# PSUM banks assigned by role, with value tiles formed one slot after their gates, in a fused attention and ReGLU kernel

## The chip, the cores and the metric

The kernel runs on one core of one Trainium2 chip. The metric is the device time of one execution in microseconds; the kernel before takes 866.84 us, the median of 3 runs (865.91 to 870.33). The profile is of one execution of its own.

The engines are named as in the profile: PE is TensorE (matmuls into PSUM, which has 8 banks here), PEld its weight loads, ACT is ScalarE, DVE is VectorE, POOL is GpSimd, SP issues the DMAs. Each engine takes its instructions in the order in which the program gives them to it, and waits for others by semaphores.

## The reference

The input `x` holds 4 batches of 12416 rows of 128. Each batch first attends from 32 fixed rows to its own rows, which gives `h` (32 × 128); then each row of `x` attends to `h`; the result goes through a gated feed-forward layer of width 1536.

```python
def mab(q, kv):
    s = scale * (q @ kv.transpose(0, 2, 1))
    s = s - s.max(-1, keepdims=True)
    a = np.exp(s)
    a /= a.sum(-1, keepdims=True) + 1e-09
    return a @ kv
h = mab(I, x)
y = mab(x, h)
...
gate = np.maximum(y @ w_gate, 0.0)
val = y @ w_val
return gate * val @ w_out
```

## The kernel before, in words

**Algebra.** The second attention and the layer's input weights are merged: for each batch the kernel computes `hgv`, that is `h @ w_gate` and `h @ w_val`, kept for 32 rows each, twice (row groups 0 and 64 the gate, 32 and 96 the value). A gate tile of 128 features by 512 rows of `x` is then one matmul of K = 32 between `hgv` and the unnormalised exps `p2`. Since the layer is a ReLU times a linear term, the softmax's denominator comes out as its square, and is applied to the finished output (L502, twice `z`).

**Tiling.** A batch is 97 tiles of 128 rows: 12 pairs of blocks (a block is 512 rows), and a rest of one tile. A pair has 12 slots, one per 128 of the 1536 features; the rest has 3 slots of four features' tiles each. A batch is therefore 147 slots, and everything that is planned has a slot number `at`.

**A slot** (L577 to L619). For both blocks `k` of the pair, TensorE forms a gate tile and a value tile (L584, four matmuls of K = 32 and N = 512, one in each of the four row groups). Then come the fillers of this slot (`fill[at]`) and some projections (`out_work`). ScalarE turns a gate tile into `g16` (ReLU, L610), VectorE multiplies `g16` by the value tile in PSUM into `gv` (L615). The list `post[at]`, follow-ups of earlier fillers on all engines, is worked off after the first block's ReLU and multiply, ahead of the second's.

**Projections.** For each block a chain of 12 matmuls (L480, `out_step`) sums `wo` times `gv` in one bank. `out_work` spends a budget of 2 projections per slot (1 in the rest), on the oldest chain, as far as its `gv` tiles are two slots old. One slot after a chain's last matmul ScalarE copies the bank to `oT` (L491), one later SP transposes it by DMA, then GpSimd scales (L502) and SP stores.

**Fillers.** `ev_s2` plans the scores of the next pair (L164, two matmuls) and a slot later their exp `p2` on ScalarE (L174); `ev_z2` the denominators (L183, four small matmuls) and a slot later their reciprocal on VectorE (L191). `plan_phase1` spreads the next batch's first attention over the slots of the current one: loads on SP, casts on GpSimd (L339), DMA transposes, first-phase scores `s1` (L359) with their exps (L369), the sums for `h` (`h_part`, L425, seven of them, followed by `sums`, `join` and `finish_h`), and the three pieces of `hgv` (L140). Batch 0 does this ahead of all slots, in a prologue of its own.

**Banks.** All PSUM tiles have one tag, `ring`, with 8 buffers of a bank each (L57). A tile takes a buffer that is free or will be the soonest in the order that the compiler plans; a matmul waits until the bank's last reader is done.

Of the kernel before, what the change touches and what calls it, by code (L numbers as in the profile page):

```python
# [9 lines left out]
FP32 = mybir.dt.float32  # L10
FP16 = mybir.dt.float16
# [6 lines left out]
def kernel(  # L18
# [20 lines left out]
    P = 128  # L39
# [47 lines left out]
    indT = constp.tile([P, M], FP16, name="indT")  # L87
    indT_ps = ring("indT_ps", [P, M], FP16)
    nc.tensor.transpose(indT_ps, ind16, eye16[:M, :M])
# [46 lines left out]

    def hgv_pe(hT, k):
        ps = ring("hgv_ps")
# [20 lines left out]
    def s2_pe(hT, xT, pr):  # L159
        ps = ring("s2_ps")  # L160
        if pr < NPAIR:
            for k in range(2):
                t0 = (2 * pr + k) * TPB
                nc.tensor.matmul(  # L164
                    ps[64 * k : 64 * k + 64, :], hT, xTs(xT, t0, TPB), start=True, stop=True
                )
# [12 lines left out]
    def z2_pe(p2, pr):  # L179
        ps = ring("z2_ps", [P, TPB, 2], FP32)  # L180
        if pr < NPAIR:
# [17 lines left out]
    xT = {}  # L199
    hT_ps = ring("hT_ps", [P, M], FP32)  # L200
    z1_ps = ring("z1_ps", [P, CT, M], FP32)
    x32s = {}
# [16 lines left out]
    for q in range(NCH):  # L219
# [16 lines left out]
        for a in range(t0, t1, 8):  # L236
            e = min(a + 8, t1)
            ps = ring("xT_ps", [P, 8, P], FP16)
            for t in range(a, e):
# [8 lines left out]
        p1s[q] = p1  # L248
        ps = ring("s1_ps", [P, CT, M], FP32)
        for t in range(t0, t1):  # L250
# [9 lines left out]
    s2 = s2_pe(hT, xT, 0)  # L260
    pss = [hgv_pe(hT, k) for k in range(3)]
    p2 = s2_exp(s2, 0)
# [38 lines left out]
    for b in range(B):  # L301
        for pr in range(NPAIR + 1):
            if (b, pr) == (0, 0):
                ev_z2(0, 0, 1)
                continue
            if pr == 0:
# [12 lines left out]

    def plan_phase1(b):  # L320
# [11 lines left out]
        for q in range(NCH):  # L332
# [21 lines left out]

            def s1(q=q, at=at + 18):
                ps = ring("s1T_ps")
                for r in range(4):
# [24 lines left out]
            if q < NQ:  # L382
                fill[at + 18].append(s1)

        at = at0 + NFF * NCH + 7

        def s1_rest(at=at):
            ps = ring("s1T_ps")
            nc.tensor.matmul(ps[0:M, 0:P], indT, xTs(s["xT"], NT - 1, 1), start=True, stop=True)
# [21 lines left out]

        at = at0 + NFF * (NQ + 2)

        def h_part(q):
            if q == 0:
                s["h_ps"] = ring("h_ps", [P, P], FP32)
            ps = s["h_ps"]
# [14 lines left out]

        for q in range(NQ + 1):
            fill[at + q].append(lambda q=q: h_part(q))

# [8 lines left out]

        post[at + NQ + 2].append(sums)

        def join():
            ps = ring("hz_ps", [P, 2, M], FP32)
            nc.tensor.matmul(ps[:, 0, :], s["hp"], stackI, start=True, stop=True)
# [5 lines left out]

            post[at + NQ + 5].append(dve)

        fill[at + NQ + 4].append(join)
        for k in range(3):

            def mk(k=k, a=at + NQ + 8 + 2 * k):
                ps = hgv_pe(s["hT"], k)
                post[a + 1].append(lambda: hgv_evac(s["hgv"], ps, k))

            fill[at + NQ + 8 + 2 * k].append(mk)

# [6 lines left out]
    def out_step(at):  # L473
# [4 lines left out]
        if i == 0:  # L478
            c["ps"] = ring("o_ps")
        nc.tensor.matmul(  # L480
# [42 lines left out]

    carry = 0.0

    def out_work(at, budget):
        nonlocal carry
        carry += budget
        while chains:
            c = chains[0]  # L530
            if c["ready"](c["i"]) > at:
                carry = min(carry, 1.0)
                return
            cost = c["w"] / BLK
            if carry < cost:
                return
            carry -= cost
            out_step(at)

    at = 0  # L540
    for b in range(B):
        for pr in range(NPAIR + 1):
            full = pr < NPAIR
            p2 = p2s[(b, pr)]
            hgv = state[b]["hgv"]
            if full:
                gvs = [st([P, NFF, BLK], FP16, "gv", 5) for _ in range(2)]
                base = at
                for k in range(2):
                    chains.append(  # L550
                        dict(
                            i=0,
                            w=BLK,
                            gv=(lambda i, g=gvs[k]: g[:, i, :]),
                            ready=(lambda i, base=base: base + i + 2),
                            key=(b, pr),
# [3 lines left out]
                        )  # L560
                    )
            else:
                gvs = [st([P, NFF, P], FP16, "gvr", 1)]
                base = at
                chains.append(
                    dict(
                        i=0,
                        w=P,
                        gv=(lambda i, g=gvs[0]: g[:, i, :]),
                        ready=(lambda i, base=base: base + i // 4 + 2),  # L570
                        key=(b, pr),
# [3 lines left out]
                    )  # L575
                )
            for s in range(NFF if full else 3):  # L577
                pss = []
                if full:
                    for k in range(2):  # L580
                        for j in range(2):
                            ps = ring("gv_ps")
                            r = 64 * k + 32 * j
                            nc.tensor.matmul(  # L584
                                ps,
                                hgv[r : r + 32, s * P : (s + 1) * P],
                                p2[r : r + 32, :],
                                start=True,
                                stop=True,
                            )  # L590
                            pss.append(ps)
                else:
                    for j in range(2):
                        ps = ring("gv_ps")
                        for i in range(4):
                            nc.tensor.matmul(
                                ps[:, i * P : (i + 1) * P],
                                hgv[32 * j : 32 * j + 32, (4 * s + i) * P : (4 * s + i + 1) * P],
                                p2[32 * j : 32 * j + 32, 0:P],
                                start=True,  # L600
                                stop=True,
                            )
                        pss.append(ps)
                for f in fill.pop(at, []):
                    f()
                out_work(at, 2.0 if full else 1.0)
                todo = post.pop(at, [])
                for k in range(len(pss) // 2):
                    g16 = st([P, BLK], FP16, "g16", 5)
                    nc.scalar.activation(out=g16, in_=pss[2 * k], func=AF.Relu)  # L610
                    if full:
                        dst = gvs[k][:, s, :]
                    else:
                        dst = gvs[0][:, 4 * s : 4 * s + 4, :].rearrange("p i c -> p (i c)")
                    nc.vector.tensor_tensor(out=dst, in0=g16, in1=pss[2 * k + 1], op=ALU.mult)  # L615
                    if k == 0:
                        for f in todo:
                            f()
                at += 1  # L619
    while chains or fill or post:  # L620
        for f in fill.pop(at, []):
            f()
        out_work(at, 12.0)
        for f in post.pop(at, []):
            f()
        at += 1
# [30 lines left out]
```

## Time and profile before

| | |
|---|---|
| Median of 3 runs | 866.84 us (865.91 to 870.33) |
| Profiled execution | 866.01 us, span 864.2 us |
| Mean granted TensorE clock | 0.960 |
| DVE busy | 736.4 us (85%), 710.7 of it in L615 |
| ACT busy | 711.1 us (82%), 621.9 of it in L610 |
| PE busy | 786.2 us (91%), 429.8 in L584 and 359.0 in L480 |
| POOL busy | 206.9 us (24%) |

The profile page gives busy time by engine, a strip of 40 equal slices of the span with the busy share in tenths (PEclk is the TensorE clock that was granted, in tenths of full speed), and the costliest groups of instructions: line, engine and operation, written tile and read tiles, count, then busy time and the mean length of one in ns, then the engine's idle time just before them and who ended most of it. In a timeline, the first number is the start and the second the length, both in us, of one or more (x4) instructions that follow each other, with the idle time before and its releaser in brackets. In the view by stretches, a line has the stretch, its length, the busy time and count, the granted clock, the DMA share and GB/s. Matmuls are pipelined and their ends are modelled, so a busy PE is not a full PE: start-to-start distances say more.

### The profile page before, as it was taken

What the parts mean: (1) busy time and instruction counts of PE and PEld (TensorE: products, weight loads), DVE (VectorE), ACT (ScalarE), POOL (GpSimd) and SP (SyncE); (2) the same over time, 40 slices, a digit from 0 to 9 for tenths busy, and PEclk for the clock granted to TensorE, in tenths of its full rate; (3) what the DMA queues carried; (4) which work ended last, traced back from release to release, by engine and by line L of the source; (5) the groups of instructions that cost most, each with busy time, mean ns of one, the idle gap of its engine ahead of it and who ended that gap; (6) DMA issues with size and microseconds to landing.
All of it is one profiled execution on the core that took longest, in us unless ns stands there. A gap on an engine that the chain in (4) does not pass through costs nothing.

```text
span 864.2 us, 14829 instructions
## 1 busy us (share of the span) xinstructions
PE 786.2 (91%) x4621; PEld 213.6 (25%) x4621; DVE 736.4 (85%) x1270; ACT 711.1 (82%) x1386; POOL 206.9 (24%) x418
## 2 busy tenths in 40 slices
PE   5789899998999998998999999999999999999995
PEld 4312222232222222222222222222122222222222
DVE  3468888888998888897899888888699999999995
ACT  4658888887898888886889888887689988888885
POOL 0203332221133233212122423222022222212213
PEclk9659999999999999998999999999699999999998
DMA  8704565211135655321115556411012112111122
GB/s 299 220 15 116 135 152 132 57 45 38 54 103 137 178 131 134 80 55 38 49 56 165 133 129 150 129 57 57 25 49 56 48 50 53 46 53 53 55 44 72
DMA packets 121167, 78.83 MB, mean 91 GB/s; under 512 B 102880, under 2 KB 105472, under 8 KB 118016
## 3 DMA queue, kind: packets, MB, share of 16 engines
q1 hardware_dynamic: 121088, 77.89, 33.7%
q8 instruction: 36, 0.59, 0.3%
q14 instruction: 43, 0.35, 0.1%
HBM read 27.80 MB, written 25.43 MB: 62 GB/s over the span
## 4 chain that ended last, share of the span: by engine, by line
PE 56%; ACT 25%; DVE 9%; issue 9%; DMA 1%; POOL 0%; SPq 0%; POOLq 0%; ACTq 0%; DVEq 0%
PE gv_ps L584 27%; PE o_ps L480 22%; ACT g L610 16%; DVE gv L615 8%; ACT oT L491 3%; ACT p L174 2%; ACT p1T L369 1%; PE z_ps L183 1%; PE s_ps L164 1%; PE s1T_ps L359 1%; PE h_ps L425 1%; PE xT_ps L240 1%; PE hgv_ps L140 1%; DMA x<-in_x_dram 1%; ACT x L224 1%
## 5 line engine op out<-in xcount | busy, mean ns | idle before, releaser
L615 DVE TENSOR_TENSOR gv<-g,gv_ps 128x512 f16<-128x512 f16 x1152 | 710.7, 680 | 92.7 <-ACT g L610 88.8
L610 ACT ACTIVATE g<-gv_ps 128x512 f16<-128x512 f32 x1164 | 621.9, 610 | 125.3 <-PE gv_ps L584 117.9
L584 PE MATMUL gv_ps<-p,hgv 32*128 32x512 f16 x2304 | 429.8, 391 | 35.3 <-ACT g L610 9.8
L480 PE MATMUL o_ps<-gv,wo 128*128 128x512 f16 x1152 | 359.0, 393 | 13.0 <-ACT g L610 11.7
L502 POOL TENSOR_SCALAR osb<-o,z2i 128x128 f32<-128x128 f16 x388 | 167.9, 447 | 620.6 <-DMA o<-oT 374.9
L584 PEld LDWEIGHTS <-hgv 32*128 32x128 f16 x2304 | 98.1, 91 | 318.1 <-issue 296.2
L480 PEld LDWEIGHTS <-wo 128*128 128x128 f16 x1200 | 76.3, 98 | 230.7 <-issue 220.5
L491 ACT CAST oT<-o_ps 128x512 f16<-128x512 f32 (+1 forms) x100 | 57.4, 574 | 1.7 <-PE o_ps L480 1.6
L339 POOL CAST x<-x 128x2048 f16<-128x2048 f32 x18 | 34.0, 1890 | 5.3 <-DMA x<-in_x_dram 2.1
L174 ACT ACTIVATE p<-s_ps 128x512 f16<-128x512 f32 x48 | 28.4, 592 | 2.6 <-PE s_ps L164 2.6
L164 PE MATMUL s_ps<-xT,hT 128*64 128x512 f16 x96 | 20.0, 412 | 2.4 <-DVE hT L134 1.6
L240 PE MATMUL xT_ps<-eye,x 128*128 128x128 f16 x97 | 10.3, 272 | 8.7 <-ACT x L224 4.8
L242 DVE COPY xT<-xT_ps 128x1024 f16<-128x1024 f16 x6 | 4.2, 692 | 13.3 <-PE xT_ps L240 13.3
L183 PEld LDWEIGHTS <-p 128*128 128x128 f16 x192 | 8.4, 97 | 20.1 <-issue 19.5
L183 PE MATMUL z_ps<-sel,p 128*128 128x2 f16 x192 | 12.0, 166 | 0.4 <-ACT g L610 0.2
L244 ACT COPY xT<-xT_ps 128x1024 f16<-128x1024 f16 x6 | 6.1, 1012 | 6.0 <-PE xT_ps L240 6.0
L164 PEld LDWEIGHTS <-hT 128*64 128x64 f16 x96 | 5.7, 107 | 21.2 <-issue 19.3
L369 ACT ACTIVATE p1T<-s1T_ps 128x512 f16<-128x512 f32 x18 | 10.9, 606 | 0.0
L240 PEld LDWEIGHTS <-x 128*128 128x128 f16 x97 | 7.8, 123 | 9.9 <-ACT x L224 6.0
L359 PE MATMUL s1T_ps<-xT,indT 128*32 128x512 f16 x72 | 7.2, 387 | 3.4 <-ACT g L610 3.4
L224 ACT CAST x<-x 128x1024 f16<-128x1024 f32 x6 | 6.2, 1038 | 4.2 <-DMA x<-in_x_dram 4.2
L191 DVE RECIPROCAL z2i<-z_ps 128x8 f32<-128x8 f32 x48 | 9.7, 201 | 0.0
(75 smaller groups left out, 113.1 us busy)
## 6 DMA issues: line engine op xcount, KB each, us to landing
x<-in_x_dram SPq DMA_DIRECT2D x24, 1024.0 KB, 5.5
out_dram<-osb SPq DMA_DIRECT2D x96, 256.0 KB, 2.0
o<-oT SPq DMA_TRANSPOSE x100, 2.4
x<-in_moe_w_gate_dram SPq DMA_DIRECT2D x1, 768.0 KB, 4.5
x<-in_moe_w_val_dram SPq DMA_DIRECT2D x1, 768.0 KB, 4.3
x<-in_moe_w_out_dram SPq DMA_DIRECT2D x1, 768.0 KB, 5.7
xT<-x SPq DMA_TRANSPOSE x18, 4.3
p1g<-p1T SPq DMA_TRANSPOSE x18, 2.4
```

The source lines that it names most:

```text
L164: nc.tensor.matmul(ps[64 * k : 64 * k + 64, :], hT, xTs(xT, t0, TPB), start=True, stop=True)
L174: nc.scalar.activation(out=p2, in_=ps, func=AF.Exp, scale=sm_scale)
L183: nc.tensor.matmul(ps[:, t, :], p2[:, t * P : (t + 1) * P], sel, start=True, stop=True)
L240: nc.tensor.transpose(ps[:, t - a, :], x16[:, t, :], eye16)
L339: nc.gpsimd.tensor_copy(out=s["x16"][:, t0:t1, :], in_=s["x32", q])
L369: nc.scalar.activation(out=p1T, in_=ps, func=AF.Exp, scale=sm_scale, accum_out=s["zp"][:, q : q + 1])
L480: nc.tensor.matmul(c["ps"][:, 0:w], wo[:, i, :], c["gv"](i), start=(i == 0), stop=(i == NFF - 1))
L491: nc.scalar.copy(out=oT[:, 0:w], in_=ps[:, 0:w])
L502: nc.gpsimd.tensor_scalar(out=osb[:, t, :], in0=o16[:, t, :], scalar1=zz, scalar2=zz, op0=ALU.mult, op1=ALU.mult,)
L584: nc.tensor.matmul(ps, hgv[r : r + 32, s * P : (s + 1) * P], p2[r : r + 32, :], start=True, stop=True,)
L610: nc.scalar.activation(out=g16, in_=pss[2 * k], func=AF.Relu)
L615: nc.vector.tensor_tensor(out=dst, in0=g16, in1=pss[2 * k + 1], op=ALU.mult)
```

## The change

The single tag of 8 banks becomes four: `g` with 3 banks for gate tiles, `v` with 3 for value tiles, `o` with 1 for a chain's sum, `m` with 1 for all else (scores, denominators, first-phase scores, h, join, hgv). In the prologue the tiles are spread over the same tags.

A slot now forms the gates of its own unit and the values of the unit before, in the order gate 0, value 0, gate 1, value 1, so the four row groups are used as before. Then the follow-ups `post` come, then projections, then fillers, then the two ReLUs of this unit and the two multiplies of the unit before.

The budget `out_work` is gone. A pair's chains have fixed slots, counted from the pair's first: the first block's 12 projections in slots 10 to 14 as 2, 2, 2, 3, 3, the second's in slots 16 to 20; slots 15 and 21 (3 and 9 of the next pair) have none. The rest's chain takes 6 and 6 in its slots 10 and 11. In slots without projections stand the scores of the next pair (slot 3, was 6) and the first-phase scores (slot 9, was 6); the denominators are in slot 6 (was 9). h's sums move by 8 slots and take 6 slots instead of 7, join and hgv follow.

The diff's core (the prologue's renamed calls are left out):

```diff
-    def ring(name, shape=None, dtype=FP32):
-        return psum.tile(shape or [P, BLK], dtype, tag="ring", bufs=8, name=name)
+    def bank(tag, name, shape=None, dtype=FP32):
+        return psum.tile(
+            shape or [P, BLK], dtype, tag=tag, bufs=3 if tag in ("g", "v") else 1, name=name
+        )
...
-            elif pr == NPAIR:
-                base = slot(b, pr - 1, 0)
-                ev_s2(b, pr, base + 4)
-                ev_z2(b, pr, base + 6)
             else:
                 base = slot(b, pr - 1, 0)
-                ev_s2(b, pr, base + 6)
-                ev_z2(b, pr, base + 9)
+                ev_s2(b, pr, base + 3)
+                ev_z2(b, pr, base + 6)
...
-            def s1(q=q, at=at + 18):
-                ps = ring("s1T_ps")
+            def s1(q=q, at=at + 21):
+                ps = bank("m", "s1T_ps")
...
-        at = at0 + NFF * NCH + 7
+        at = at0 + NFF * NCH + 9
...
-        at = at0 + NFF * (NQ + 2)
+        at = at0 + NFF * (NQ + 2) + 8
...
-        for q in range(NQ + 1):
-            fill[at + q].append(lambda q=q: h_part(q))
+        for q, d in enumerate((0, 1, 1, 2, 3, 4, 5)):
+            fill[at + d].append(lambda q=q: h_part(q))
...
-        post[at + NQ + 2].append(sums)
+        post[at + 6].append(sums)
...
-            post[at + NQ + 5].append(dve)
-
-        fill[at + NQ + 4].append(join)
+            post[at + 13].append(dve)
+
+        fill[at + 12].append(join)
...
-            def mk(k=k, a=at + NQ + 8 + 2 * k):
+            def mk(k=k, a=at + 13 + 2 * k):
...
-            c["ps"] = ring("o_ps")
+            c["ps"] = bank("o", "o_ps")
...
+    def plan_chain(first, counts, **c):
+        chains.append(dict(i=0, **c))
+        for d, n in enumerate(counts):
+            steps[first + d] += n
...
+                        plan_chain(
+                            base + 10 + 6 * k,
+                            (2, 2, 2, 3, 3),
...
+    def form(t, j):
+        ps = t["ps", j] = bank("gv"[j], "gv"[j] + "_ps")
+        for cols, s, p2, hgv in t["mm"][j]:
+            nc.tensor.matmul(ps[:, cols], hgv[:, s * P : (s + 1) * P], p2, start=True, stop=True)
+
+    at = 0
+    todo_units = units()
+    before = []
+    while True:
+        unit = next(todo_units, [])
+        if not (unit or before or fill or post or chains):
+            break
+        for k in range(2):
+            if k < len(unit):
+                form(unit[k], 0)
+            if k < len(before):
+                form(before[k], 1)
+        for f in post.pop(at, []):
+            f()
+        for _ in range(steps.pop(at, 0)):
+            out_step(at)
         for f in fill.pop(at, []):
             f()
...
+        for t in unit:
+            g16 = t["g16"] = st([P, BLK], FP16, "g16", 5)
+            nc.scalar.activation(out=g16, in_=t["ps", 0], func=AF.Relu)
+        for t in before:
+            nc.vector.tensor_tensor(out=t["dst"], in0=t["g16"], in1=t["ps", 1], op=ALU.mult)
+        before = unit
         at += 1
```

`units()`, a new generator, yields per slot the one or two units of the loops that the old code ran through: two per slot in a pair, one in the rest.

More of the change, by code (lines that the diff above doesn't have):

```diff
@@ L159, in s2_pe @@
     def s2_pe(hT, xT, pr):
-        ps = ring("s2_ps")
+        ps = bank("m", "s2_ps")
         if pr < NPAIR:
@@ L260 @@
     s2 = s2_pe(hT, xT, 0)
-    pss = [hgv_pe(hT, k) for k in range(3)]
+    pss = [hgv_pe(hT, k, "g") for k in range(3)]
     p2 = s2_exp(s2, 0)
@@ L522, in out_step, with units @@
         post[at + 1].append(evac)
[L524 to L552, printed above, removed]
+    steps = defaultdict(int)
+    def plan_chain(first, counts, **c):
+        chains.append(dict(i=0, **c))
+        for d, n in enumerate(counts):
+            steps[first + d] += n
+    def units():
+        for b in range(B):
+            for pr in range(NPAIR + 1):
+                base = slot(b, pr, 0)
+                p2, hgv = p2s[(b, pr)], state[b]["hgv"]
+                if pr < NPAIR:
+                    gvs = [st([P, NFF, BLK], FP16, "gv", 5) for _ in range(2)]
+                    for k in range(2):
+                        plan_chain(
+                            base + 10 + 6 * k,
+                            (2, 2, 2, 3, 3),
                             w=BLK,
                             gv=(lambda i, g=gvs[k]: g[:, i, :]),
-                            ready=(lambda i, base=base: base + i + 2),
                             key=(b, pr),
@@ L560 @@
                         )
[L561 to L567, printed above, removed]
-                        w=P,
-                        gv=(lambda i, g=gvs[0]: g[:, i, :]),
-                        ready=(lambda i, base=base: base + i // 4 + 2),
+                    for s in range(NFF):
+                        yield [
+                            dict(
+                                mm=[
+                                    [(slice(0, BLK), s, p2[r : r + 32, :], hgv[r : r + 32, :])]
+                                    for r in (64 * k, 64 * k + 32)
+                                ],
+                                dst=gvs[k][:, s, :],
+                            )
+                            for k in range(2)
+                        ]
+                else:
+                    gv = st([P, NFF, P], FP16, "gvr", 1)
+                    plan_chain(
+                        base + 10,
+                        (6, 6),
+                        w=P,
+                        gv=(lambda i, g=gv: g[:, i, :]),
                         key=(b, pr),
@@ L575 @@
                     )
[L576 to L589, printed above, removed]
-                            )
[L591 to L619, printed above, removed]
@@ L620 @@
-    while chains or fill or post:
+                    for s in range(3):
+                        yield [
+                            dict(
+                                mm=[
+                                    [
+                                        (
+                                            slice(i * P, (i + 1) * P),
+                                            4 * s + i,
+                                            p2[r : r + 32, 0:P],
+                                            hgv[r : r + 32, :],
+                                        )
+                                        for i in range(4)
+                                    ]
+                                    for r in (0, 32)
+                                ],
+                                dst=gv[:, 4 * s : 4 * s + 4, :].rearrange("p i c -> p (i c)"),
+                            )
+                        ]
```

33 lines of the change are left out of this document (15 added, 18 removed).

## The prediction, made before the change was run

> **What bounds the kernel now.** I read the page first: the busy shares, the clock line, the two costliest groups.
>
> ```profile
> span 864.2 us, 14829 instructions
> ...
> PE 786.2 (91%) x4621; PEld 213.6 (25%) x4621; DVE 736.4 (85%) x1270; ACT 711.1 (82%) x1386; POOL 206.9 (24%) x418
> ...
> PEclk9659999999999999998999999999699999999998
> ...
> L615 DVE TENSOR_TENSOR gv<-g,gv_ps 128x512 f16<-128x512 f16 x1152 | 710.7, 680 | 92.7 <-ACT g L610 88.8
> L610 ACT ACTIVATE g<-gv_ps 128x512 f16<-128x512 f32 x1164 | 621.9, 610 | 125.3 <-PE gv_ps L584 117.9
> ...
> L369 ACT ACTIVATE p1T<-s1T_ps 128x512 f16<-128x512 f32 x18 | 10.9, 606 | 0.0
> ```
>
> VectorE's multiply L615 is the largest item, and it idles 92.7 us, nearly all of it for the ReLU (L610), which itself idles 117.9 us for the gate and value matmuls (L584). So no engine is full, and each one waits for another. The next question is where. I cut the span at the first multiply of a pair of blocks (24 multiplies, 12 slots) and asked for the busy time of L615 in each stretch (the count includes multiplies that reach over the edges).
>
> ```profile
> 37.20:57.60 20.40, 15.39 (x25) 0.50 0.30 79
> 112.10:129.10 17.00, 14.72 (x25) 1.00 0.68 151
> 382.90:401.30 18.40, 15.29 (x26) 1.00 0.21 44
> 401.30:422.00 20.70, 15.08 (x26) 0.84 0.15 39
> 453.40:455.40 2.00, 1.91 (x4) 1.00 0.03 8
> 741.80:757.60 15.80, 14.62 (x25) 1.00 0.18 51
> 852.00:864.20 12.20, 1.89 (x4) 0.80 0.26 73
> ```
>
> A pair takes 15.8 us in the last batch and 17.0 beside the next batch's first phase; 20.4 at the start, where the clock column says 0.50; 18.4 and 20.7 where the next batch's h is made. What is left are a batch's three rest slots (2.0 us) and the end (12.2, the last three rest slots among it). Inside one plain pair, VectorE's timeline shows that the loss sits in a few slots:
>
> ```profile
> 757.04 3.67 DVE L615 TENSOR_TENSOR gv<-g,gv_ps 128x512 f16<-128x512 f16 x6
> 760.92 5.47 DVE L615 TENSOR_TENSOR gv<-g,gv_ps 128x512 f16<-128x512 f16 x9 [0.21 <-ACT g L610]
> 766.55 0.69 DVE L615 TENSOR_TENSOR gv<-g,gv_ps 128x512 f16<-128x512 f16 x1 [0.16 <-ACT g L610]
> 768.01 3.68 DVE L615 TENSOR_TENSOR gv<-g,gv_ps 128x512 f16<-128x512 f16 x6 [0.78 <-ACT g L610]
> 771.61 0.20 DVE L191 RECIPROCAL z2i<-z_ps 128x8 f32<-128x8 f32 x1
> 771.73 2.43 DVE L615 TENSOR_TENSOR gv<-g,gv_ps 128x512 f16<-128x512 f16 x4
> ```
>
> Nine multiplies in a row take 5.47 us and one takes 0.69, so they follow each other every (5.47 − 0.69)/8 = 0.60 us. Outside the three gaps VectorE is the bound: 24 × 0.5975 = 14.34, plus 0.13 for the reciprocal (771.73 − 768.01 is 3.72, six multiplies are 3.59), so **14.47 us is a pair's floor**. Against it stand 15.8 and 17.0. ScalarE and TensorE around the largest gap show why it opens:
>
> ```profile
> 763.18 2.06 ACT L610 ACTIVATE g<-gv_ps 128x512 f16<-128x512 f32 x4 [0.33 <-PE gv_ps L584]
> 765.92 0.60 ACT L610 ACTIVATE g<-gv_ps 128x512 f16<-128x512 f32 x1 [0.67 <-PE gv_ps L584]
> 766.41 0.59 ACT L174 ACTIVATE p<-s_ps 128x512 f16<-128x512 f32 x1
> 766.89 0.59 ACT L491 CAST oT<-o_ps 128x512 f16<-128x512 f32 x1
> 767.35 1.12 ACT L610 ACTIVATE g<-gv_ps 128x512 f16<-128x512 f32 x2
> ```
> ```profile
> 763.43 0.38 PE L480 MATMUL o_ps<-gv,wo 128*128 128x512 f16 x1
> 763.74 0.95 PE L584 MATMUL gv_ps<-p,hgv 32*128 32x512 f16 x4
> 764.62 0.41 PE L164 MATMUL s_ps<-xT,hT 128*64 128x512 f16 x2
> 764.96 0.60 PE L480 MATMUL o_ps<-gv,wo 128*128 128x512 f16 x2
> 765.50 0.39 PE L584 MATMUL gv_ps<-p,hgv 32*128 32x512 f16 x4
> 765.85 0.59 PE L480 MATMUL o_ps<-gv,wo 128*128 128x512 f16 x2
> ```
>
> Two things meet. First, the four gate and value matmuls of a slot start together and take 0.35 us to the next group when all banks are free (765.50 to 765.85), but 0.88 when not (763.74 to 764.62): a value tile is formed with its gate, holds its bank until ReLU and multiply are both done, and TensorE, which keeps its order, stands before the fourth matmul with the scores and projections queued behind it. So the next gates come late and ScalarE idles 0.67 us. Second, right after that idle ScalarE has an exp and an eviction in one slot, both between its two ReLUs, and the second multiply waits for all of it.
>
> **The change part by part.** No matmul, ReLU or multiply is added or dropped; bank choice and order change. I first ask whether the new order can hold 0.60 us per multiply, by the margins.
>
> *Latencies, from the rows above:* matmul start to ReLU start 0.42 (765.50 to 765.92); ReLU start to multiply start 0.63 (765.92 to 766.55); two ScalarE passes 0.46 to 0.49 apart; a projection about 0.21 after the one before (two last 0.59 to 0.60, one 0.38), two projections to the next gates 0.54 (764.96 to 765.50), the score group 0.34 (764.62 to 764.96).
>
> *Value banks.* With three banks a value matmul waits for the multiply three before it. If a unit's two multiplies start at 0 and 0.60, the bank of the first comes free at −1.80 + 0.69 = −1.1 and its matmul must start by −0.42; for the second it is −0.5 and +0.18. After the second, TensorE needs 0.35 + 0.54 = 0.89 in a slot of two projections (2, 2, 2, 3, 3, 0 are laid out), so it reaches the next slot's matmuls at +0.39; they must start by 1.20 − 0.42 = +0.78. Margin 0.39, with three projections 0.18, and in the slot without projections, where the scores now lie, more. So TensorE just holds the pace, the three-projection slots on a thin margin. What is queued behind a blocked value matmul is the next gate: that is the wait which the change adds, and ScalarE is who would feel it.
>
> *ScalarE's lead.* The gate of the next unit goes out with those matmuls, at −0.81 (three projections: −0.60); its ReLU starts at −0.39 and is needed at 1.20 − 0.63 = +0.57. The lead is 0.96 us, or 0.75 after three projections. A slot costs ScalarE 2 × 0.495 = 0.99 of 1.20, so it regains 0.21 per slot. Eviction and exp now fall in neighbouring slots instead of one: they take 0.46 + 0.48 − 0.42 = 0.52 of the lead, leaving 0.2. Six slots on, eviction and first-phase exp (L369, taken at its full 0.61) leave 0.1. Nothing is late by this sum, but margins of 0.1 to 0.2 are as large as my reading errors: I charge **0.2 us per pair** between 0 and the no-lead case below, nearer 0 because each step came out positive. A pair is 14.67.
>
> *The chain bank.* A second chain can't start until the first is evicted. Last projection in one slot, first of the next chain two slots later: 2.0 us by the times above. The eviction needs 0.42 to see the sum and 0.6 to finish, and ScalarE can take it some 0.5 after that sum is ready. Margin about half a microsecond; cost nothing, covered by the empty slot.
>
> *The misc bank.* Scores, z, first-phase scores, h parts, join and hgv share one bank, and each is evicted one slot after it is filled; the lists put no two in one slot and neighbours three slots apart, h's stay ending with the sums just before the next scores. New is that hgv's first piece is filled in the slot in which VectorE makes hT: TensorE stands there for about a slot.
>
> *Transfers.* Loads, casts, transposes, stores keep their slot offsets while slots shrink from 1.42 to 1.22. First-phase scores move from 7 to 10 slots after their transpose is issued (9.9 us before, 12.2 after); the transposes of their exps on SP's queue move with them, and the h parts that read these by eight slots. SP and GpSimd get the same instructions in 14% less time; the DMA share of 0.68 would become 0.79. I charge nothing.
>
> *Changeovers.* Around the making of h, pairs now cost 18.4 + 20.7, which is 2.6 + 4.9 = 7.5 over two plain ones. VectorE's own extra work (sums, hT, one hgv eviction) stays, some stalls stay, h parts are closer packed: between 2 and 7.5 per batch, I take 5.
>
> *Start.* No projection runs in the first ten slots, and the clock is 0.50 there. At that clock a slot with two projections takes 1.51 us on TensorE:
>
> ```profile
> 62.80 0.61 PE L584 MATMUL gv_ps<-p,hgv 32*128 32x512 f16 x4
> 63.35 1.03 PE L480 MATMUL o_ps<-gv,wo 128*128 128x512 f16 x2
> 64.31 0.87 PE L584 MATMUL gv_ps<-p,hgv 32*128 32x512 f16 x4
> ```
>
> Without projections 0.55 suffice, so ten slots can run at VectorE's pace; then some slots lose 0.3 to 0.7 each until the clock rises: 3 us, between 1 and 9 (two pairs at 20.4 against 15.8 now).
>
> *Rest slots.* They get 2, 3 and 3 projections. By the plain slot's times TensorE needs 0.89 + 1.10 + 1.10 = 3.1 us for the three, more than VectorE's three multiplies, instead of 2.0. At the end a chain of 12 and the rest chain still follow each other: 12.2 becomes 14.4, 1.1 for the slots and 1.1 for a last chain that waits for the bank of the one before (0.42 + 0.6).
>
> **Sum.** 37.2 to the first multiply (unchanged) + 48 × 14.67 = 704.2 + 3 × 3.1 = 9.3 for rests + 14.4 for the last rest and the end + 3 × 5 = 15 for changeovers + 3 for the start = 783.1. The profiled execution took 866.0 for a span of 864.2, so +1.8; and the median, 866.84, lies 0.8 above it: **786 us**, 9% below 866.84.
>
> **Rivals.**
> *No lead.* If gates come so late that ScalarE has no lead, each extra pass stalls VectorE: per pair 2 evictions and an exp, less 0.21 per slot, 0.8 us, and 1.2 in the 21 pairs with first-phase exps. That is 27 × 0.8 + 21 × 1.2 = 47 in place of 9.6: 823. For it: thin margins, and today's ScalarE idle has this very form. Against it: every step still came out positive.
> *The chain bank decides (slower).* If ScalarE reaches the eviction late, the first projection of each chain holds TensorE, and the next gates behind it. It is free until the eviction is 0.5 us later than drawn. If ScalarE gets to it 1.5 later, behind two ReLUs and an exp, each of 96 chains holds TensorE for 1.0: 786 + 96 = 882; it decides from 0.84 per chain, where the gain of 81 is gone. Against it: the eviction stands ahead of its slot's ReLUs.
> *Half clock (slower).* TensorE's clock falls to half during the pairs, through the empty slots and bank waits. By the half-clock rows above (0.55 for a gate group, 0.96 for two projections and the switch, so 0.43 and 0.10) and 0.6 for the scores, a pair would take 12 × 0.55 + 24 × 0.43 + 10 × 0.10 + 0.6 = 18.5 us; with half of the 48 pairs so, 24 × 3.83 adds 92: 878, and it decides from 21 pairs. Against it: the clock column is 1.00 in plain pairs, which wait for banks too, and 0.84 only at a changeover.
> The Trainium skill, "TensorE: Matmul & The Clock Gate", section "A second HAM failure mode: psum-queue depth-cycling", speaks against this change: cycling through a few PSUM banks leaves small idles between matmul groups, from which the clock oscillates. By that rule the time would be this rival's 878; the trace, with 1.00 in pairs that cycle eight banks, does not follow it so far.
> *Not noticed.* The gaps return elsewhere in equal size: 864, for which I see no row.
>
> **How the numbers follow.** Forecast 0.70, no lead 0.17, chain bank 0.06, half clock 0.05, no change 0.02. A measurement of this kernel can tell about 0.5% (4.3 us). Faster takes the first two and the mild end of the next two, 0.88; same 0.03; slower 0.09. The forecast's own range runs from 786 − 9.6 − 9 − 2 = 765 (no stall left, changeovers 2, start 1) to 786 + 14 + 7.5 = 808 (0.5 us left per pair, changeovers 7.5). The whole range reaches on to no lead with changeovers at 7.5, 823 + 7.5 = 830, and leaves out the slower cases.
>
> **What would show it.** Right: multiplies in runs of 20 and more at 0.60 us, VectorE's idle before L615 (now 92.7) under 25 us, plain pairs at 14.5 to 14.9, clock 1.00 in them. Wrong: gaps for ReLU in the slots of eviction and exp (no lead), a projection that waits for the eviction (chain bank), clock under 1.00 in plain pairs.

## The result, and the profile after

The changed kernel takes 773.7 us, the median of 4 runs (773.01 to 773.93), against 868.59 for the kernel before in 4 runs (865.91 to 874.36): a ratio of 0.890, with a 95% interval of 0.885 to 0.895. The forecast was 786, in a range of 765 to 830. The profiled execution took 773.68 us for a span of 771.5.

From the page of the changed kernel, the lines that answer to those of before (the multiply is L618 now, the ReLU L616):

```profile
span 771.5 us, 15512 instructions
...
PE 709.3 (92%) x4621; PEld 210.3 (27%) x4621; DVE 722.4 (94%) x1270; ACT 695.4 (90%) x1386; POOL 207.2 (27%) x418
...
PEclk9759999999999999999998999999999999999998
...
L618 DVE TENSOR_TENSOR gv<-g,v_ps 128x512 f16<-128x512 f16 x1152 | 696.2, 679 | 7.0 <-PE v_ps L594 5.8
L616 ACT ACTIVATE g<-g_ps 128x512 f16<-128x512 f32 x1164 | 615.6, 626 | 40.2 <-PE g_ps L594 20.1
```

The counts are those of before, and VectorE's busy time fell by only 14 us (busy time is a union, and multiplies that follow each other overlap). What went is its idle time ahead of the multiply: 92.7 us became 7.0. VectorE is busy 94% of the span and is the bound in most pairs. Its timeline over two pairs of the last batch of the changed kernel:

```profile
645.71 0.20 DVE L194 RECIPROCAL z2i<-z_ps 128x8 f32<-128x8 f32 x1
645.83 14.41 DVE L618 TENSOR_TENSOR gv<-g,v_ps 128x512 f16<-128x512 f16 x24
660.15 0.20 DVE L194 RECIPROCAL z2i<-z_ps 128x8 f32<-128x8 f32 x1
660.27 14.41 DVE L618 TENSOR_TENSOR gv<-g,v_ps 128x512 f16<-128x512 f16 x24
```

24 multiplies without a gap, then the reciprocal: 660.27 − 645.83 = 14.44 us per pair, the floor that the prediction worked out as 14.47. ScalarE beside the next pair:

```profile
668.41 1.08 ACT L616 ACTIVATE g<-g_ps 128x512 f16<-128x512 f32 x2 [0.33 <-PE g_ps L594]
669.38 0.59 ACT L489 CAST oT<-o_ps 128x512 f16<-128x512 f32 x1
669.85 1.12 ACT L616 ACTIVATE g<-g_ps 128x512 f16<-128x512 f32 x2
670.81 0.65 ACT L177 ACTIVATE p<-s_ps 128x512 f16<-128x512 f32 x1
671.29 4.14 ACT L616 ACTIVATE g<-g_ps 128x512 f16<-128x512 f32 x8
675.61 1.09 ACT L616 ACTIVATE g<-g_ps 128x512 f16<-128x512 f32 x2 [0.18 <-PE g_ps L594]
```

Eviction and exp stand in neighbouring slots, and ScalarE runs without a pause from 668.41 until its lead is regained at 675; only then does it wait again, for a gate. The multiplies never notice. The view by stretches, cut as before at the first multiply of a pair, shows where time above the floor is left:

```profile
37.70:53.60 15.90, 14.80 (x25) 0.50 0.38 101
53.60:68.40 14.80, 14.58 (x25) 0.98 0.30 67
97.30:111.80 14.50, 14.46 (x26) 1.00 0.69 179
155.20:170.00 14.80, 14.58 (x26) 1.00 0.19 56
170.00:186.30 16.30, 14.62 (x26) 1.00 0.21 64
215.80:218.30 2.50, 1.94 (x3) 1.00 0.28 105
218.30:234.20 15.90, 14.82 (x25) 0.81 0.52 147
234.20:249.20 15.00, 14.64 (x25) 0.97 0.59 146
653.00:667.40 14.40, 14.37 (x26) 1.00 0.19 56
756.60:771.50 14.90, 0.00 (x0) 0.75 0.21 59
```

Pairs beside the first phase are at the floor too (14.5, were 17.0). Above it are the first pair at half clock, the making of h (14.8 and 16.3, were 18.4 and 20.7), the pair after it (14.9, 186.3 to 201.2, not in the view), the rest slots (2.5, were 2.0), the first two pairs after them, where the granted clock is 0.81 and 0.97, and the end: 14.9 us without a multiply, where before it was 864.2 − 853.9 = 10.3 (the last multiply of before ends at 853.89).

### The profile page after: what moved, and what is told of

Read it like the earlier page. It is cut to its first block, busy times and chain, and to the rows that moved or that the text cites. A ratio compares the mean times of both kernels' runs of the same rounds, so it can differ in the third digit from the quotient of the medians.

```text
span 771.5 us, 15512 instructions
## 1 busy us (share of the span) xinstructions
PE 709.3 (92%) x4621; PEld 210.3 (27%) x4621; DVE 722.4 (94%) x1270; ACT 695.4 (90%) x1386; POOL 207.2 (27%) x418
## 4 chain that ended last, share of the span: by engine, by line
PE 51%; ACT 20%; issue 12%; DMA 8%; DVE 4%; POOL 3%; SPq 0%; ACTq 0%; POOLq 0%; DVEq 0%
PE o_ps L478 23%; PE g_ps L594 18%; ACT g L616 14%; PE v_ps L594 7%; DMA xT<-x 3%; DVE gv L618 3%; DMA o<-oT 3%; ACT oT L489 3%; POOL osb L500 2%; ACT p L177 1%; POOL x L337 1%; ACT p1T L367 1%; PE xT_ps L243 1%; DMA p1g<-p1T 1%; PE h_ps L423 1%
## 5 line engine op out<-in xcount | busy, mean ns | idle before, releaser
L618 DVE TENSOR_TENSOR gv<-g,v_ps 128x512 f16<-128x512 f16 x1152 | 696.2, 679 | 7.0 <-PE v_ps L594 5.8
L616 ACT ACTIVATE g<-g_ps 128x512 f16<-128x512 f32 x1164 | 615.6, 626 | 40.2 <-PE g_ps L594 20.1
L594 PE MATMUL v_ps<-p,hgv 32*128 32x512 f16 (+1 forms) x1200 | 368.3, 381 | 4.7 <-DVE gv L618 2.8
L478 PE MATMUL o_ps<-gv,wo 128*128 128x512 f16 x1152 | 336.6, 389 | 0.3 <-ACT oT L489 0.3
L594 PE MATMUL g_ps<-p,hgv 32*128 32x512 f16 (+1 forms) x1200 | 303.3, 381 | 28.8 <-ACT g L616 26.5
L594 PEld LDWEIGHTS <-hgv 32*128 32x128 f16 x2400 | 91.0, 91 | 287.6 <-issue 276.4
L177 ACT ACTIVATE p<-s_ps 128x512 f16<-128x512 f32 x48 | 30.8, 641 | 2.7 <-PE s_ps L167 2.6
L186 PEld LDWEIGHTS <-p 128*128 128x128 f16 x192 | 11.5, 97 | 12.4 <-issue 2.3
L167 PEld LDWEIGHTS <-hT 128*64 128x64 f16 x96 | 5.3, 107 | 20.1 <-issue 18.4
L618 DVE TENSOR_TENSOR gvr<-g,v_ps 128x512 f16<-128x512 f16 x12 | 8.1, 674 | 2.2 <-PE g_ps L594 1.2
```

The source lines that it names most:

```text
L167: nc.tensor.matmul(ps[64 * k : 64 * k + 64, :], hT, xTs(xT, t0, TPB), start=True, stop=True)
L177: nc.scalar.activation(out=p2, in_=ps, func=AF.Exp, scale=sm_scale)
L186: nc.tensor.matmul(ps[:, t, :], p2[:, t * P : (t + 1) * P], sel, start=True, stop=True)
L478: nc.tensor.matmul(c["ps"][:, 0:w], wo[:, i, :], c["gv"](i), start=(i == 0), stop=(i == NFF - 1))
L594: nc.tensor.matmul(ps[:, cols], hgv[:, s * P : (s + 1) * P], p2, start=True, stop=True)
L616: nc.scalar.activation(out=g16, in_=t["ps", 0], func=AF.Relu)
```

## The experiments

Theory A is the prediction's account: values that sit in a bank while ScalarE works couple TensorE to ScalarE, and extra passes in one slot then stall VectorE. The change has three parts that can be taken apart: the **delay** (values and multiplies one slot late), the **plan** (fixed slots for chains and fillers, follow-ups ahead of the ReLUs), and the **roles** (banks by tag). A run without a range is one execution; the kernel before took 860 to 874 us beside them, so a difference of a few us against it says nothing, and smaller differences below are read from the traces.

**The delay undone, banks by role and plan kept** (`e1`).

```diff
         unit = next(todo_units, [])
+        before = unit
...
-        before = unit
         at += 1
```

> Banks by role and the fixed plan stay; a value tile is formed with its own gate again, one slot earlier than in the changed kernel. Theory A (the gain comes from value tiles no longer sitting in a bank while ScalarE works): a value then holds its bank from 1.05 us before its multiply; with three value banks the next gates come 0.3 us late in slots of two projections and 0.45 in slots of three, so pairs take 16 to 17.5 us instead of 14.47 and the whole 850 to 920 us. Theory B (the fixed slots and the banks by role carry the gain, the delay does not matter): within 10 us of 773.7.

944.36 us: slower than the kernel before by 9%, and past A's range. A pair at full clock takes 16.9, as A has it; in that pair TensorE stands before the second value matmul of most slots (in the whole run 232 times by more than 0.15 us, in 576 slots):

```profile
111.56 0.37 PE L594 MATMUL g_ps<-p,hgv 32*128 32x512 f16 x1
112.28 0.37 PE L594 MATMUL v_ps<-p,hgv 32*128 32x512 f16 x1 [0.35 <-DVE gv L619]
112.59 0.61 PE L478 MATMUL o_ps<-gv,wo 128*128 128x512 f16 x2
113.12 0.38 PE L594 MATMUL g_ps<-p,hgv 32*128 32x512 f16 x1
```

At 16.92 all 48 pairs would take 812 us; they take 870. Most of that difference goes with the clock, which now falls again and again over the whole run. The page's line:

```profile
PEclk9579998898879898988978998989877887887978
```

So banks by role don't pay without the delay; they cost (one ring without the delay, `e3` below, takes 798.66).

**The roles undone, delay and plan kept** (`e2`).

```diff
         return psum.tile(
-            shape or [P, BLK], dtype, tag=tag, bufs=3 if tag in ("g", "v") else 1, name=name
+            shape or [P, BLK], dtype, tag="ring", bufs=8, name=name
         )
```

> Value tiles one slot late and the fixed plan stay; all tiles share one tag of eight banks again. Theory A: the delay already frees the banks in time, so 773 to 790 us and plain pairs under 14.8. Theory C (the roles matter: in a shared ring a gate is given a bank that a multiply frees late): gaps return, pairs at 15 or more, 800 us or more.

765.66 us, under A's range and 8 us **less** than the changed kernel. Theory C falls: no gap returns. The stretches of this run that answer to the changed kernel's pair at 218.3, to the one at 186.3 (after the making of h) and to its rest slots:

```profile
217.30:231.80 14.50, 14.46 (x25) 1.00 0.49 142
186.40:200.80 14.40, 14.36 (x25) 1.00 0.16 38
215.40:217.30 1.90, 1.85 (x3) 1.00 0.30 113
```

They take 14.5 in place of 15.9, 14.4 in place of 14.9 and 1.9 in place of 2.5, and the clock doesn't fall there; pairs beside the first phase are slower by 0.15 each (14.62 for 14.47). Where the roles cost shows in TensorE's idle time ahead of the gate matmuls, from the page of the changed kernel and the page of this run:

```profile
L594 PE MATMUL g_ps<-p,hgv 32*128 32x512 f16 (+1 forms) x1200 | 303.3, 381 | 28.8 <-ACT g L616 26.5
L594 PE MATMUL g_ps<-p,hgv 32*128 32x512 f16 (+1 forms) x1200 | 287.0, 380 | 4.8 <-DVE gv L618 3.8
```

With three gate banks TensorE waits 26.5 us for ReLUs to free one; with one ring that wait is gone.

**Delay and roles undone, the plan alone** (`e3`): both edits above together.

> Both undone: one tag of eight banks, values with their own gates; only the fixed slots of chains and fillers and the earlier follow-ups stay. Theory A: most of the loss is back, pairs of 15.5 to 17, 825 to 880 us; what it gains against 867 is the share of the plan alone (exp and eviction no longer in one slot, worth up to 0.5 us per pair or 24 us). Theory B: near 774.

798.66 us: neither theory's range. The plan alone is worth 66 us of the 91 that separate 864.19 (the kernel before beside this run) from 773.7, far more than the 24 that I gave to separating exp and eviction. Most pairs are at 14.9 to 15.2. Against `e2`, which has the same plan and the same ring, this run lacks the delay alone: 798.66 − 765.66 = 33 us is what the delay is worth on top of the plan.

**The delay in the kernel before** (`e9`): old slots of fillers, one ring.

```diff
-                            ready=(lambda i, base=base: base + i + 2),
+                            ready=(lambda i, base=base: base + i + 3),
...
+        for k in range(2):
+            if k < len(now):
+                form(now[k], 0)
+            if k < len(before):
+                form(before[k], 1)
+        for f in fill.pop(at, []):
+            f()
+        out_work(at, budget)
...
+            for t in now[k : k + 1]:
+                g16 = t["g16"] = st([P, BLK], FP16, "g16", 5)
+                nc.scalar.activation(out=g16, in_=t["ps", 0], func=AF.Relu)
+            for t in before[k : k + 1]:
+                nc.vector.tensor_tensor(out=t["dst"], in0=t["g16"], in1=t["ps", 1], op=ALU.mult)
```

> The kernel before with one change: a value tile is formed, and its multiply issued, one slot after its gate (a chain's projections become ready a slot later with it). One tag of eight banks, the old slots of fillers, the budget for projections, follow-ups between the two ReLUs all stay. Theory A (the delay gives ScalarE a lead of 0.75 us or more, which also covers an exp and an eviction in one slot, 0.95 us less 0.42 of slack): 770 to 800 us. Rival (the plan carries most of the gain; without it the delay is worth only the 33 us that it is worth on top of the plan): 825 to 840 us.

778.95 us, in A's range: 87 us less than the kernel before. But this is not the delay alone. With `ready` a slot later, a chain ends a slot later, and its eviction with it, while the exps stay where they were. In before, exp and eviction follow each other in one slot (766.41 and 766.89 in the prediction's rows); here two ReLUs stand between them, so they are in neighbouring slots, as in the changed kernel. ScalarE (first) and VectorE:

```profile
686.38 0.59 ACT L174 ACTIVATE p<-s_ps 128x512 f16<-128x512 f32 x1
686.86 1.09 ACT L588 ACTIVATE g<-g_ps 128x512 f16<-128x512 f32 x2
687.82 0.62 ACT L491 CAST oT<-o_ps 128x512 f16<-128x512 f32 x1
```
```profile
679.67 10.84 DVE L590 TENSOR_TENSOR gv<-g,v_ps 128x512 f16<-128x512 f16 x18
690.44 0.20 DVE L191 RECIPROCAL z2i<-z_ps 128x8 f32<-128x8 f32 x1
```

18 multiplies run through; ScalarE's lead covers both passes. Whether it would cover them in one slot, as A says, this run doesn't show. Delay with moved evictions (87) and plan (66) overlap: together, in one ring, they bring about 98 (864.19 − 765.66).

**Only the exps moved, in the kernel before** (`e10`).

```diff
-                ev_s2(b, pr, base + 6)
+                ev_s2(b, pr, base + 3)
...
-            def s1(q=q, at=at + 18):
+            def s1(q=q, at=at + 21):
...
-                fill[at + 18].append(s1)
+                fill[at + 21].append(s1)
```

> The kernel before with two numbers changed: the scores of the next pair 3 slots earlier (their exp in slot 4, was 7) and the first-phase scores 3 later (their exp in slot 10, was 7), so that no exp falls in the slot of an eviction (2 and 7 in the trace of before). If two or three extra ScalarE passes in one slot open the large gaps: plain pairs from 15.84 to about 15.1 us, pairs beside the first phase from 17.03 to about 15.6, total 805 to 835 us. Rival (the gaps come from banks that values hold, whatever lies in the slot): 850 to 867 us.

826.72 us, 39 us less than the 865.74 of before: two numbers carry more than half of the plan's worth. VectorE in a plain pair of this run shows one gap of 0.29 where before had 0.21, 0.16 and 0.78:

```profile
721.83 6.34 DVE L615 TENSOR_TENSOR gv<-g,gv_ps 128x512 f16<-128x512 f16 x10
728.46 7.29 DVE L615 TENSOR_TENSOR gv<-g,gv_ps 128x512 f16<-128x512 f16 x12 [0.29 <-ACT g L610]
```

The pair takes 15.1, as expected, and one beside the first phase 15.9 (expected 15.6).

**Follow-ups between the ReLUs again** (`e4`): the changed kernel with `post` worked off after the first ReLU and multiply, as before.

```diff
-        for f in post.pop(at, []):
-            f()
+        todo = post.pop(at, [])
...
+            if k == 0:
+                for f in todo:
+                    f()
```

> As the changed kernel, but follow-ups (eviction, exp, reciprocal, hgv copies) stand after the slot's first ReLU and first multiply, as in the kernel before, in place of ahead of both. Theory A with ScalarE's lead of 0.75 to 0.96 us: the second ReLU comes 0.5 us later relative to the first, the lead covers it, 770 to 785 us. Rival (position of the extra passes was half of the gain, there is no lead): each of some 3.5 passes per pair stalls VectorE 0.3 to 0.5, 1 to 1.7 us per pair, 820 to 855 us.

778.47 us. With the lead there, the position of a pass within its slot costs 0.07 us in a plain pair (14.54 and 14.51, for 14.47 and 14.44), some 2 us in all; about 3 more lie in the pairs around the making of h, where the clock falls too.

**Two value banks** and **two gate banks**, the freed one given to chains (`e5`, `e6`).

```diff
-            shape or [P, BLK], dtype, tag=tag, bufs=3 if tag in ("g", "v") else 1, name=name
+            shape or [P, BLK], dtype, tag=tag, bufs=dict(g=3, v=2, o=2, m=1)[tag], name=name
```

> As the changed kernel, but 3 banks for gates, 2 for values, 2 for chains, 1 misc. By the margins (a value matmul waits for the multiply two before it, which ends 0.74 after its start; TensorE then needs 0.89 us to the next slot's matmuls, 1.10 with three projections, and the multiply follows 0.42 after): 2.65 us per two slots, 1.33 per slot with two projections, 1.43 with three, 1.2 without, so pairs of 16.1 and about 855 us. Rival (two banks hold the pace, the third is spare): within 8 us of 773.7.

> As the changed kernel, but 2 banks for gates, 3 for values, 2 for chains, 1 misc. A gate matmul waits for the ReLU two before it. By the margins ScalarE then needs 1.23 us per slot with two projections and 1.33 with three, and each extra pass (about 3 per pair) adds 0.5 more: pairs of 15.1 to 16.5, 805 to 870 us. Rival (ScalarE's lead does not come from the third gate bank): within 8 us of 773.7.

923.68 and 849.94 us. With two value banks a pair at full clock takes 16.7 (forecast 16.1), and the whole comes out 69 us above the forecast: 48 × 0.64 = 31 of that is the pair itself, and the clock, which falls often (mean 0.89), brings most of the rest. With two gate banks most pairs take 15.6 to 17.1, and the whole is inside the range. With roles, the third bank of each is needed; for these two the expectations, worked out from the prediction's margins, have the right sign and roughly the right size.

**No empty slot** (`e7`): twelve projections as six times two.

```diff
-                            (2, 2, 2, 3, 3),
+                            (2, 2, 2, 2, 2, 2),
```

> As the changed kernel, but a chain's 12 projections are spread as 2 in each of 6 slots, so that no slot is left empty between chains and the one chain bank must be evicted within the slot. Theory A: the copy is ready 2.05 us after the slot's first matmul and the next chain's first projection would be issued at 1.85, a wait of 0.2 us that the value margin of 0.39 covers; the slots with scores need 1.23 us of TensorE, a loss of some 0.1: 770 to 788 us. Rival (the empty slot is what makes one chain bank enough): TensorE waits 0.6 us or more at each of 96 chains, 830 us or more.

776.89 us (774.48 to 781.05 in 4 runs; 0.897 of before, 0.890 to 0.904). Most pairs take 14.5 to 14.6. TensorE does wait for the eviction, as this run's page shows (last two fields), but 4.5 us in 96 chains:

```profile
L478 PE MATMUL o_ps<-gv,wo 128*128 128x512 f16 x1152 | 351.5, 388 | 12.5 <-ACT oT L489 4.5
```

The rival, that one chain bank holds TensorE, falls even without the empty slot. What does cost in the profiled execution is a transfer: one pair (489.2 to 507.8) takes 18.6 us, because TensorE waits up to 3.1 us for the DMA transpose of `x` ahead of first-phase scores.

**More matmuls where TensorE has little to do** (`e8`). In slots 7 and 9 of a batch's first pair, from the second batch on, five matmuls whose results nothing reads:

```diff
         if i == 0:
             c["ps"] = bank("o", "o_ps")
+            if w < BLK and c["b"] < B - 1:
+                for _ in range(2):
+                    nc.tensor.matmul(
+                        c["ps"], wo[:, 0, :], xTs(state[c["b"] + 1]["xT"], 0, TPB), start=True, stop=True
+                    )
...
+        if SPB < at < B * SPB and at % SPB == 9:
+            ps = bank("m", "w_ps")
+            for _ in range(3):
+                nc.tensor.matmul(
+                    ps, wo[:, 0, :], xTs(state[at // SPB]["xT"], 0, TPB), start=True, stop=True
+                )
```

> As the changed kernel, with five more matmuls per batch, whose results nothing reads, in slots 7 and 9 of the first pair of the second, third and fourth batch, where the plan leaves TensorE little to do and the clock fell to half for 6.83 us at 228 and 409 us. If too little work there is the cause: the clock stays at 1.00 in these places, the two first pairs go from 15.89 to about 14.7 us and the second ones from 14.9 to 14.5, total 769 to 771 us. Rival (the fall comes from the h sums and the waits at hgv some 40 us earlier, or from the rest slots): the clock falls there as before and the time is 773 to 776.

770.83 us (769.53 to 771.18 in 4 runs). The clock stays up in both first pairs, which answer to 15.90 at 0.81 above:

```profile
219.00:233.80 14.80, 14.64 (x26) 1.00 0.48 142
399.00:413.80 14.80, 14.64 (x25) 1.00 0.53 152
```

So here more work on TensorE makes the kernel faster, and the making of h isn't what brings the fall. But light slots alone don't bring it either: `e2` has the same ones and keeps 1.00, as `e11` below does, and so does the first pair of the fourth batch of the changed kernel. Something else decides there, which no run isolates.

**The best version: one ring, and a shorter end** (`e11`). The end of the changed kernel is SP's queue:

```profile
756.10 1.19 SPq L493 DMA_TRANSPOSE o<-oT  x1
760.53 0.34 SPq L510 DMA_DIRECT2D out_dram<-osb  x1
760.96 1.22 SPq L493 DMA_TRANSPOSE o<-oT  x1
765.31 0.34 SPq L510 DMA_DIRECT2D out_dram<-osb  x1
765.74 1.13 SPq L493 DMA_TRANSPOSE o<-oT  x1
768.69 0.34 SPq L510 DMA_DIRECT2D out_dram<-osb  x1
```

Each transpose stands behind the store of the chain before, and that store waits for GpSimd. In before, two of them went out with no store between:

```profile
853.59 3.41 SPq L495 DMA_TRANSPOSE o<-oT  x2
```

The edit, on top of that of `e2`, moves the last pair's two stores back in the order:

```diff
-                    post[at + 5].append(store)
+                    last = c["key"] == (B - 1, NPAIR - 1)
+                    post[at + ((9, 7)[c["k"]] if last else 5)].append(store)
```

> As the changed kernel, but all tiles share one tag of eight banks (as in the run that took 765.66 us), and for the last pair alone the stores come later in SP's order, so that the transposes of the last two chains are not queued behind stores that wait for GpSimd. If that queue is what makes the end 15 us long: 3 to 5 us less than 765.66, so 760.5 to 763 us. Rival (GpSimd or the transposes themselves set the end): 764 to 766 us.

761.05 us (759.89 to 761.41 in 6 runs): 0.878 of before, 0.875 to 0.881, and 4.6 below `e2`. SP's queue at the end of this run, where again two transposes follow each other with no store between:

```profile
747.17 4.21 SPq L493 DMA_TRANSPOSE o<-oT  x2
751.61 0.40 SPq L510 DMA_DIRECT2D out_dram<-osb  x1
752.12 1.13 SPq L493 DMA_TRANSPOSE o<-oT  x1
754.56 0.81 SPq L510 DMA_DIRECT2D out_dram<-osb  x2
```

## Why the prediction was right, and where its steps were off

**The floor and its reach were right.** A pair's floor was put at 14.47 us; 30 of the 48 pairs take 14.4 to 14.55. The 0.2 us per pair (9.6 in all) that I charged for thin margins was not needed: every margin that came out positive held, down to one of 0.1. The tests with one bank less show that the same arithmetic also says when it breaks.

**The cause was half right.** The prediction named two things that meet in before, banks held by waiting values and extra passes in one slot. For the second, `e10` is the test: the exps moved out of the evictions' slot bring 39 us. For the first, `e2` against `e3` is the test: forming values later brings 33 on top of the plan. That the loss comes about through the banks that values hold is in part argued. The prediction read the wait before the fourth matmul of a slot as one at a value's bank; the profile of before puts TensorE's waits at the gate and value matmuls down to ReLUs, 9.8 us, and 0.5 to multiplies, so most banks that it waited for had held gates:

```profile
L584 PE MATMUL gv_ps<-p,hgv 32*128 32x512 f16 x2304 | 429.8, 391 | 35.3 <-ACT g L610 9.8
```

Values that hold banks longer may leave gates fewer; forming them later also puts the next gates ahead of them in TensorE's order, and no run separates the two. What the prediction took for granted is the part in the change's title: banks by role. They bring nothing; with delay and plan in place they cost 8 us, and without the delay they make the kernel slower than before. My question was whether three and three banks hold the pace, not whether eight shared ones hold it better. The margins looked at the value banks and not at the gate banks, and there the changed kernel waits: 28.8 us ahead of gate matmuls, 4.7 ahead of value matmuls.

**The sum, term by term** (predicted, then measured): to the first multiply 37.2, 37.7. The 48 pairs with changeovers and start 704.2 + 15 + 3 = 722.2, then 708.7, of which 48 × 14.47 = 694.6 is the floor, some 8.5 the making of h (predicted 15: mostly VectorE's own extra work is left), 1.8 the start, and some 4 the clock falls after the rest slots, which no term of mine had. The four groups of rest slots 12.4, then 10.2. From the last multiply to the end 14.4 − 3.1 = 11.3, then 15.0: this is the step that failed. I counted the chain that waits for its bank, but not the DMA queue: with chains at fixed slots the last two end later and farther apart, and their transposes queue on SP behind stores. I had written that SP gets the same instructions and charged nothing; `e11` shows the place to be worth 4.6 us. Together 783.1 became 771.6: the pairs and rest slots came out 15.7 below their terms, the end and the start 4.2 above, so part of the closeness is errors that offset each other.

**The rivals.** *No lead*: not seen; ScalarE recovers its lead in each pair. *The chain bank*: not seen, and in `e7`, where a chain ends in the slot just before the next one begins, TensorE waits 4.5 us in all: the bank has more slack than the half microsecond that I gave it. *Half clock*: seen, but not where I put it: 0.81 and 0.97 in the first two pairs of the second and third batch, about 4 us in all. In plain pairs that cycle three banks per role the clock is 1.00. The Trainium skill's section "A second HAM failure mode: psum-queue depth-cycling" (page "TensorE: Matmul & The Clock Gate") would have the clock oscillate there, which the trace doesn't show. It fits `e1` and `e5`, where TensorE waits for a multiply before value matmuls 232 and 216 times by more than 0.15 us, and the mean clock was 0.87 and 0.89. In this case cycling through few banks was not enough for the clock to fall; which waits are enough is not shown, for pairs of `e1` with such waits also ran at 1.00 (16.92 us).

**What stays open.** Why the clock doesn't fall in the first pair of the fourth batch of the changed kernel, whose slots are as light, wasn't tested. Nor was it tested which part of the plan beside the moved exps brings its other 27 us, nor what the delay brings with the evictions left in the exps' slot.

## What to carry to other kernels

When two operands of one instruction come out of PSUM, form the one that nobody works on first as late as its reader allows: here that was worth 33 us on top of the plan, and naming the banks cost 8. Before splitting a shared pool by role, run the new order with the pool shared. And when work is moved toward the end, follow it to the last store: the queue order of the few final DMAs can cost more than a bank wait.

## What the runs showed of the hardware that was not expected

- The clock can fall without a long wait of TensorE: slots 6 to 9 of a batch's first pair, about 5 us that hold little beside their gates and values but the rest's twelve small projections, were followed by a granted clock of half in the second and third batch, not in the fourth, and five superfluous matmuls per batch (`e8`) kept it at 1.00 with a net gain of some 3 us. One ring (`e2`) kept it too, without them.
- A slowdown by bank waits is amplified by the clock. With two value banks 48 pairs of 16.74, the time of one at full clock, would be 803.5 us; the measured pairs take 854. Some 10 of the difference is the making of h and the start (an estimate: 8.5 and 1.8 in the changed kernel), most of the rest goes with the falls of the clock.
- Back to back on 128x512 tiles from PSUM, ScalarE's ReLU follows itself every 0.50 us ((4.14 − 0.63)/7 from the row at 671.29) and VectorE's multiply every 0.60 ((14.41 − 0.68)/23).
